# A kernel whose task order is written out as a table: the table is replaced by another one

## The chip, the cores and the metric

One core of a Trainium2 chip runs the whole program in one launch. The metric is the device time of the program in microseconds (us). Its engines are TensorE (PE, with its weight loads shown as PEld), VectorE (DVE), ScalarE (ACT), GpSimd (POOL) and SyncE (SP); each runs its own instructions strictly in the order in which they were written, and they wait for one another by semaphores.

## The reference

The output is a gated mix of two branches over a sequence of 2048 rows of 640 channels: local attention with a window of 8 keys at a stride of 2, and a long convolution whose kernel comes from a diagonal state space model.

```python
g = sigmoid((x * gate_w).sum(-1, keepdims=True))
# a: 32 heads of 20; each query sees keys at pos - 0, 2, .., 14
q, k, v = split(x @ wqkv)
logits = where(idx >= 0, einsum("bhsd,bhswd->bhsw", q, kg) * scale, -1e9)
a = (einsum("bhsw,bhswd->bhsd", softmax(logits), vg)) @ wo
# b: K = Re sum_n C_n dB_n exp(dt A_n l), 192 states per channel; FFT convolution of x with K
K = einsum("dn,dnl,dn->dl", Cc, exp(logdA[:, :, None] * l), dB).real
b = irfft(rfft(x, 4096) * rfft(K, 4096))[:2048] + x * Dskip
out = g * a + (1 - g) * b
```

## The kernel before, in words

The work is cut into 1578 tasks, each of which issues a handful of instructions on one engine. The program first builds the list of tasks with what each depends on, in a fixed numbering. Then `Plan.order` reads a table of numbers, `ORDER`, and gives the order in which the tasks are written out; there are two such tables, "main" and "tail". A number is the step from the last task's place in the list to the next one's, and a letter behind it names the engine where a task can run on either ACT (A) or DVE (D). Since every engine runs in order, the table is the whole schedule: no scheduler changes it, and the tile framework adds the semaphores that the order needs.

```python
for x in ORDER[self.name].split():
    at += int(x.rstrip("ADSG"))
    t = self.tasks[at]
    t.eng = x[-1] if x[-1] in "ADSG" else next(iter(t.dur))
    out.append(t)
```

What the tasks do, with the lines of the profile:

- Start, to about 55 us. DVE and ACT turn the model's parameters into digit pieces (tiles `pc`, L661), SP stores them to the scratch `Sprm` and reads them back as `L` tiles (L766). PE transposes x in ten tasks (L204); each is evicted from PSUM (tile `ar`) to `bufA` by ACT (L507) or DVE (L509). PE projects q, k and v in 60 groups of five matmuls (L311), each evicted from one of two PSUM buffers (`tb`) into `qA`, `kA`, `prj`, `pv` or `vst`. The gate's 80 small matmuls (L219) need all transpositions.
- Kernel generation, ten chunks. PE computes arguments (L801, tile `ar`), ACT takes Sin (L816) and Exp (L818), DVE multiplies them (L838 and L840, tiles `pt` and `qq`), PE sums the products into the chunk (L856, `kps`), and an eviction puts it into `E` ("the E eviction", L507). After five chunks a half of the kernel is expanded (`nxt`, `X`), stored to `Kx` and loaded as `kc`.
- Attention, eight slices of 256 queries, numbered 0 to 7, woven into that. DVE multiplies q by shifted k (L375, `prod`), PE sums (L381, `lg`), DVE takes the row maximum (L397 to L401), ACT Exp (L409), DVE divides (L417, L418); SP writes the result to `aS` and spreads it as `asb` (L428). POOL loads the values of a slice as `vc` in two transfers (L368) from the scratch `vS` (L344), DVE multiplies them (L449, `pv`), PE gathers (L456), and the output projection (L480) is scaled by the gate on eviction ("the gate eviction", L489 on ACT, L491 on DVE).
- Transforms. `Usb`, which is x in another layout, is loaded by POOL in eight transfers (L1004). Ahead of each but the first stands a small POOL copy that reads what the transfer before wrote (L1003, tile `pace`), so the eight run one after another. `Usb` takes the buffer in which `prj` was, so the first must wait until `prj` is no longer read. Then PE transforms `Usb` and `kc` (L1300, L1319).
- Tail, from about 267 us: the spectra (L1073), their products on DVE (L1101, L1104), the inverse transform (L1134, L1164), the mix (L1170 to L1178) and the stores (L1191).

`vc` has two buffers, which are handed out in turn in the order in which the loads are issued; a load waits until DVE has read the buffer's last contents.

## Time and profile before

| | |
|---|---|
| median of 3 runs | 336.16 us (335.34, 336.16, 339.4) |
| span of the profiled execution | 335.4 us (the page lists no other time for it) |
| PE busy | 285.5 us |
| DVE busy | 294.2 us |
| ACT busy | 293.4 us |
| POOL busy | 62.3 us |
| moved by DMA | 45.68 MB, mean 136 GB/s |

The profiled execution's span is 0.06 us above the lowest run and 0.8 us below the median. Three engines are each busy for 85 to 88% of the span, so no engine's total says what bounds the kernel. What an engine's row says of a stage must be read from that stage: its idle time, and what ended it. A PE that is busy is not a PE at its peak, since the ends of its matmuls are modelled.

### The profile page before, as it was taken

To read this page: it belongs to the slowest core of one execution; us is meant where nothing else is said; L and a number is where in the kernel's file an instruction comes from. 1 tells how busy PE (TensorE), PEld (TensorE's weight loads), DVE (VectorE), ACT (ScalarE), POOL (GpSimd) and SP (SyncE) were. 2 spreads that over 40 slices of the span, in tenths; PEclk is the share of its full clock that TensorE was granted. 3 is DMA by queue.
4 is the path that set the end of the run, shared out by engine and by line. 5 is a ranking of instruction groups with operands and counts; after the bars stand their busy time and mean duration, and the time that the engine had idled before them with its cause. 6 is when DMAs were issued, how large, how long until landed. Compare 5 with 4: busy or idle time off the path is not lost. (4 is left out here: it accounts for less than half of the span.)

```text
span 335.4 us, 11982 instructions
## 1 busy us (share of the span) xinstructions
PE 285.5 (85%) x5181; PEld 171.0 (51%) x5214; DVE 294.2 (88%) x401; ACT 293.4 (87%) x433; POOL 62.3 (19%) x94
## 2 busy tenths in 40 slices
PE   0367999997899999999998799999999899996850
PEld 0334563444445555445554344556677676665740
DVE  1997988798989999999999979999686799999881
ACT  1789736999899999999999799999987889998990
POOL 8700043020005000101412341211040000000062
PEclk9999999999999999999999989999999999999985
DMA  8984435437107110524874887365565527666056
GB/s 253 356 264 113 119 91 159 86 91 170 26 9 153 27 24 8 149 62 141 199 190 119 186 208 161 93 118 124 154 207 221 180 64 216 159 123 100 4 136 182
DMA packets 45975, 45.68 MB, mean 136 GB/s; under 512 B 25098, under 2 KB 39738, under 8 KB 45922
## 3 DMA queue, kind: packets, MB, share of 16 engines
q1 hardware_dynamic: 39928, 27.90, 30.3%
q0 software_dynamic: 5248, 16.39, 20.2%
q8 instruction: 41, 0.67, 0.9%
q10 hardware_dynamic: 746, 0.61, 0.6%
q14 instruction: 12, 0.10, 0.1%
HBM read 30.88 MB, written 14.01 MB: 134 GB/s over the span
## 5 line engine op out<-in xcount | busy, mean ns | idle before, releaser
L311 PE MATMUL tb<-bufA 128*128 128x512 bf16 x267 | 73.5, 391 | 4.2 <-issue 1.4
L816 ACT ACTIVATE big<-ar 128x740 bf16<-128x740 int16 (+1 forms) x72 | 56.7, 858 | 1.4 <-PE ar L801 1.2
L818 ACT ACTIVATE big<-ar 128x848 bf16<-128x848 f32 x60 | 50.1, 905 | 0.2
L801 PE MATMUL ar<-Rarg,L 64*128 64x212 bf16 (+4 forms) x600 | 46.5, 253 | 3.5 <-ACT big L816 1.9
L449 DVE TENSOR_TENSOR pv<-vc,asb 128x2048 bf16<-128x2048 bf16 x40 | 48.2, 1217 | 0.3 <-PE tb L456 0.3
L311 PEld LDWEIGHTS <-bufA 128*128 128x128 bf16 x300 | 31.2, 122 | 28.5 <-issue 12.3
L856 PEld LDWEIGHTS <-pt 128*32 128x32 bf16 (+1 forms) x2560 | 25.3, 92 | 35.7 <-issue 33.2
L856 PE MATMUL kps<-qq,pt 128*32 128x21 bf16 (+1 forms) x2560 | 36.6, 173 | 6.0 <-issue 5.1
L838 DVE TENSOR_TENSOR pt<-big 128x1024 bf16<-128x1024 bf16 x48 | 32.8, 701 | 4.3 <-ACT big L816 2.2
L801 PEld LDWEIGHTS <-L 64*128 64x128 bf16 x600 | 20.8, 94 | 25.2 <-issue 22.4
L480 PE MATMUL tb<-wo_sb,oT 128*128 128x320 bf16 x160 | 29.9, 306 | 0.2
L507 ACT ACTIVATE sp_u<-fp 128x640 bf16<-128x640 f32 x31 | 23.9, 953 | 0.8 <-PE fp L1073 0.8
L375 DVE TENSOR_TENSOR prod<-prj 128x2048 bf16<-128x2048 bf16 x20 | 24.0, 1218 | 0.2 <-PE lg L381 0.2
L375 DVE TENSOR_TENSOR prod<-qA,kA 128x2048 bf16<-128x2048 bf16 x20 | 23.9, 1217 | 0.2 <-PE lg L381 0.2
L507 ACT ACTIVATE sp_k<-fp 128x640 bf16<-128x640 f32 x29 | 22.6, 969 | 1.1 <-PE fp L1073 1.1
L456 PE MATMUL tb<-pv,ind 128*64 128x512 bf16 (+1 forms) x192 | 23.2, 353 | 0.0
L368 POOL DMA_DIRECT2D vc<-vS x16 | 11.5, 723 | 59.0 <-DVE pv L449 55.0
L840 DVE TENSOR_TENSOR qq<-big 128x1344 bf16<-128x1344 bf16 x24 | 21.2, 883 | 0.0
L1191 POOL DMA_DIRECT2D out_dram<-ot x14 | 7.7, 558 | 72.3 <-DVE ot L1173 72.3
L1073 PEld LDWEIGHTS <-PHI 128*128 128x128 bf16 x160 | 15.5, 97 | 8.1 <-issue 1.1
L489 ACT ACTIVATE ga<-tb,g_sb 128x320 bf16<-128x320 f32 x29 | 15.6, 550 | 3.4 <-PE tb L480 3.1
L480 PEld LDWEIGHTS <-oT 128*128 128x128 bf16 x160 | 13.1, 98 | 7.1 <-issue 3.1
(171 smaller groups left out, 547.9 us busy)
## 6 DMA issues: line engine op xcount, KB each, us to landing
vc<-vS POOLq DMA_DIRECT2D x16, 327.5 KB, 6.4
xn<-in_A_x_dram SPq DMA_DIRECT2D x4, 640.0 KB
gaS<-ga SPq DMA_DIRECT2D x8, 320.0 KB
Usb<-in_A_x_dram POOLq DMA_DIRECT2D x8, 320.0 KB, 5.7
gaF<-gaS SPq DMA_DIRECT2D x8, 320.0 KB
bufA<-in_A_wqkv_dram SPq DMA_DIRECT2D x3, 800.0 KB
Sprm<-pc SPq DMA_DIRECT2D x10, 240.0 KB
L<-Sprm SPq DMA_DIRECT2D x76, 30.0 KB
```

Source lines behind the costliest of these rows:

```text
L311: nc.tensor.matmul(ppf, self.wq[:, which, kt, e::5], self.xT[:, c0 // 1024, kt, c0 % 1024:c0 % 1024 + SC], start=(kt == 0), stop=(kt == NK ...
L375: nc.vector.tensor_tensor(b[e][:], q[:, e, o:o + C].unsqueeze(1).to_broadcast([128, W, C]), win(k[:, e, :], o, W, DIL, C), ALU.mult)
L449: nc.vector.tensor_tensor(o, vw, b["asb"][:].unsqueeze(2).to_broadcast(sh), ALU.mult)
L456: nc.tensor.matmul(b["op", e][64 * a:64 * a + 64, 0:n, :], ind[:, 32:96], b["pv", e][:, w, a, 0:n, :], start=(w == 0), stop=(w == 3), skip ...
L480: nc.tensor.matmul(apf[:, :320], b["oT"][:, e, i * 128:(i + 1) * 128], wo_sb[:, e, hf * 320:(hf + 1) * 320], start=(e == 0), stop=(e == 4))
L507: nc.scalar.activation(o, i, ACT.Identity)
L801: nc.tensor.matmul(ar[:, g2, a0:a0 + ncol], L[rows, sb, gv, l0:l0 + 128], R[rows, c0:c0 + ncol], start=True, stop=True, tile_position=(64 ...
L816: nc.scalar.activation(d_[:, :, s0 * QW:s1 * QW], ar[:].bitcast(I16)[:, :, 0:2 * (s1 - s0) * QW:2], ACT.Sin, scale=SCL)
L818: nc.scalar.activation(dst[:, gp::2].rearrange("p g s n -> p g (s n)"), ar[:, :, 0:2 * EW], ACT.Exp)
L838: nc.vector.tensor_tensor(pt[:, :, k, :], gg[:, :, ::-1] if k else gg, e1, ALU.mult)
L840: nc.vector.tensor_tensor(qq[:], trg[:, :, KI:].rearrange("p a (v m) -> p a v m", v=2), exq[:, :, KI:].unsqueeze(2).to_broadcast([128, 32, ...
L856: nc.tensor.matmul(kps[32 * g:32 * g + 32, h, NM * ql:NM * ql + NM], pt[rows, k, v, :], qq[rows, k, v, :], start=(g not in started), stop= ...
```

## The change

Both tables are replaced. The numbers of a row say nothing to a reader; the first row of "main" and of "tail" stand for all:

```diff
 ORDER = {"main": (
-    "7 -7 15 -14 1 1166 -1164 56 -57 3 2 -3 6 1 1 39 -43 1 51A -8A -25 -14 2 38 1D 1 1A -32 33 1A -42 1 69 1 -57 72 -56 57 "
+    "15 37 1116 -1161 -7 1 3 1 6 -9 1 3 48 -46 1 44 -41 48 -5 -42 48 -5 -42 2 -6 18 30 -1 2 28 1 -65 1 7 1 40 -55 5 25 42D "
...
 ), "tail": (
-    "3 1A 7 1A -7 1D 1 6 1A -6D 1 1A 10 -5 1A 1 1A 3 13 1D -13 1 1 2 1A 3 1A -3 1A -4 11 1A 6 -11 1A 11 -6 1A 1 1A -41 1 "
+    "0 13 -12 10 -4 5D 2 -6D -5 1 1 1D 14 -11 1 11 -6 1 1 1 8 1D 1 1 5 1 -33 139 -105 1 -7 1 1 1 -14 19 1 1 125 -112 -31 1 "
...
```

The tasks, their instructions, tiles and bytes are the same, and so are 19 loads of activation tables on ACT. The new table is six lines shorter, so that a line of the program has a number 6 lower in the change (L509 becomes L503). In "main", 30 evictions and parameter steps go from ACT to DVE and 23 come from DVE to ACT; in "tail", 4 go and 3 come. Three places:

DVE ahead of its first attention products (L375, then L369), from the last parameter pieces on. Before:

```order
L661 TENSOR_TENSOR pc<-at,t_144 128x960
L661 TENSOR_TENSOR pc<-t_144,t_143 128x960
L509 CAST bufA<-ar 128x1024 x3
L509 CAST kA<-tb 128x512
L375 TENSOR_TENSOR prod<-qA,kA 128x2048 x2
```

In the change:

```order
L655 TENSOR_TENSOR pc<-t_144,t_143 128x960
L503 CAST kA<-tb 128x512 x2
L503 CAST qA<-tb 128x512
L328 MEMSET kA 128x5x7
L503 CAST qA<-tb 128x512
L369 TENSOR_TENSOR prod<-qA,kA 128x2048 x2
```

The three transposition evictions (`bufA<-ar`) are gone to ACT, as is a fourth one earlier; four projection evictions stand there instead of one.

POOL between the loads of the later slices' `vc` and of `Usb`. The numbers behind the names tell the buffers apart: `vc_4160`, `vc_4812` and `vc_5174` are those of slices 4, 5 and 6. Before:

```order
L368 DMA vc_4160<-vS_68 64x10x262 x2
L1003 COPY pace_77<-Usb_3673 32x2
L1004 DMA Usb_3673<-in_A_x_dram 32x32x160
L1003 COPY pace_77<-Usb_3673 32x2
L1004 DMA Usb_3673<-in_A_x_dram 32x32x160
L938 DMA kc_4305<-Kx_178 128x2560
L1003 COPY pace_77<-Usb_3673 32x2
L1004 DMA Usb_3673<-in_A_x_dram 32x32x160
L368 DMA vc_4812<-vS_68 64x10x262 x2
L1003 COPY pace_77<-Usb_3673 32x2
L1004 DMA Usb_3673<-in_A_x_dram 32x32x160
L368 DMA vc_5174<-vS_68 64x10x262 x2
```

In the change, where `vc_4676` is slice 4's, `vc_5097` slice 5's, `vc_5107` slice 7's and `vc_5578` slice 6's, from the fifth load of `Usb` on:

```order
L362 DMA vc_4676<-vS_68 64x10x262 x2
L997 COPY pace_77<-Usb_3956 32x2
L998 DMA Usb_3956<-in_A_x_dram 32x32x160
L997 COPY pace_77<-Usb_3956 32x2
L998 DMA Usb_3956<-in_A_x_dram 32x32x160
L997 COPY pace_77<-Usb_3956 32x2
L998 DMA Usb_3956<-in_A_x_dram 32x32x160
L1001 DMA omF_76<-omS_58 32x32
L987 DMA PHI_4864<-c_phi 128x1536
L932 DMA kc_4862<-Kx_178 128x2560
L1001 DMA omF_76<-omS_58 32x32 x2
L362 DMA vc_5097<-vS_68 64x10x262 x2
```

Slice 5's values now come behind all eight loads of `Usb` and five other transfers. Behind them follow `vc_5107` (slice 7) and `vc_5578` (slice 6), in this order.

DVE at the end of the kernel products, around the last value product of slice 5 (`pv` with 128x8x256) and the first of slice 6. Before:

```order
L417 RECIPROCAL rs_5293<-lg_4734 128x64
L418 TENSOR_TENSOR at_5218<-at_5218,rs_5293 128x512
L449 TENSOR_TENSOR pv_104<-vc_4812,asb_5029 128x8x256
L838 TENSOR_TENSOR pt_5470<-bufA_78,big_601 128x32x32 x2
L840 TENSOR_TENSOR qq_5471<-bufA_78,big_601 128x1344
L449 TENSOR_TENSOR pv_104<-vc_5174,asb_5335 128x4x512 x3
```

In the change:

```order
L443 TENSOR_TENSOR pv_104<-vc_5097,asb_4857 128x8x256
L832 TENSOR_TENSOR pt_5227<-big_585 128x32x32
L834 TENSOR_TENSOR qq_5228<-big_585 128x1344
L832 TENSOR_TENSOR pt_5301<-big_585 128x32x32 x2
L834 TENSOR_TENSOR qq_5302<-big_585 128x1344
L832 TENSOR_TENSOR pt_5355<-bufA_78,big_585 128x32x32 x2
L834 TENSOR_TENSOR qq_5356<-bufA_78,big_585 128x1344
L411 RECIPROCAL rs_5409<-lg_5047 128x64
L412 TENSOR_TENSOR at_5264<-at_5264,rs_5409 128x512
L485 TENSOR_SCALAR ga_5407<-tb_5347,g_sb_65 128x320
L443 TENSOR_TENSOR pv_104<-vc_5578,asb_5160 128x4x512 x4
```

The last softmax division (`rs`, `at`) stands behind the kernel products instead of ahead of them, and the work between slice 5's last value product and slice 6's first has grown from one kernel product to nearly three.

88 rows, old and new, of the table ORDER are left out of this document.

## The prediction

> **What bounds the kernel now.** I read the page first, then the span cut into its stages, then the groups of instructions with their idle time, and last the timelines of VectorE (DVE), ScalarE (ACT), TensorE (PE) and GpSimd (POOL) at the places where something waits.
>
> ```profile
> span 335.4 us, 11982 instructions
> PE 285.5 (85%) x5181; PEld 171.0 (51%) x5214; DVE 294.2 (88%) x401; ACT 293.4 (87%) x433; POOL 62.3 (19%) x94
> 55.00:100.00 45.00, 40.80 (x772) 20.38 (x785) 38.66 (x56) 42.70 (x60) 4.03 (x6) 1.00 0.38 85
> 100.00:188.00 88.00, 84.02 (x1933) 44.62 (x1950) 85.50 (x119) 87.85 (x134) 15.68 (x25) 1.00 0.46 110
> 188.00:196.00 8.00, 5.64 (x99) 2.15 (x96) 5.75 (x7) 5.58 (x10) 3.50 (x3) 0.79 0.74 180
> 196.00:232.00 36.00, 34.61 (x956) 19.63 (x952) 35.15 (x45) 35.67 (x53) 9.52 (x13) 1.00 0.57 132
> 232.00:267.00 35.00, 32.77 (x326) 24.68 (x326) 27.81 (x40) 30.42 (x45) 4.37 (x8) 1.00 0.63 200
> ```
>
> The columns of a stage are its length and the busy time of PE, weight loads, DVE, ACT and POOL. No engine is the bound alone. From 55 to 232 ACT is busy 171.8 of 177 us (42.70 + 87.85 + 5.58 + 35.67) and DVE 165.1. What an order can win lies in DVE's idle time before 100, in the hole at 188 to 196, and in the stage 232 to 267, where PE has the least idle time (35.00 - 32.77 = 2.2). The chain that ended last covers only the final stores and says nothing of the change.
>
> Where DVE waits before 100, and the hole at 191:
>
> ```profile
> 44.89 0.69 DVE L509 CAST kA<-tb 128x512 bf16<-128x512 f32 x1 [0.72 <-PE tb L311]
> 49.06 0.69 DVE L509 CAST prj<-tb 128x512 bf16<-128x512 f32 x1 [0.43 <-PE tb L311]
> 62.31 0.69 DVE L509 CAST prj<-tb 128x512 bf16<-128x512 f32 x1 [1.33 <-PE tb L311]
> 76.74 1.34 DVE L509 CAST prj<-tb 128x512 bf16<-128x512 f32 x2 [1.73 <-PE tb L311]
> 94.44 0.69 DVE L509 CAST prj<-tb 128x512 bf16<-128x512 f32 x1 [1.16 <-PE tb L311]
> 191.39 0.27 PE L856 MATMUL kps<-qq,pt 128*32 128x21 bf16 x15 [2.36 <-issue]
> 194.26 0.71 DVE L838 TENSOR_TENSOR pt<-big 128x1024 bf16<-128x1024 bf16 x1 [2.25 <-ACT big L816]
> ```
>
> The bracket is the idle time just before and who ended it. DVE stands still because an eviction of a projection was put on it before PE had made the projection. The hole is PE's own (nothing that the profile shows held it) and DVE loses 2.25 us by it. The order cannot aim at that hole; I leave it in.
>
> **The change part by part.** The instructions and bytes are the same, so each term is work that goes to another engine or a wait that goes or comes. The prices of what changes engine:
>
> ```profile
> L509 DVE CAST prj<-tb 128x512 bf16<-128x512 f32 x10 | 6.8, 688 | 5.8 <-PE tb L311 5.8
> L491 DVE TENSOR_SCALAR ga<-tb,g_sb 128x320 bf16<-128x320 f32 x3 | 1.6, 546 | 1.0 <-ACT big L507 1.0
> L509 DVE CAST bufA<-ar 128x1024 bf16<-128x1024 f32 x4 | 4.7, 1215 | 0.0
> L507 ACT ACTIVATE prj<-tb 128x512 bf16<-128x512 f32 x15 | 9.3, 636 | 1.4 <-PE tb L311 1.4
> L489 ACT ACTIVATE ga<-tb,g_sb 128x320 bf16<-128x320 f32 x29 | 15.6, 550 | 3.4 <-PE tb L480 3.1
> L507 ACT ACTIVATE E<-kps 128x336 bf16<-128x336 f32 x10 | 4.7, 471 | 1.3 <-PE kps L856 1.3
> L507 ACT ACTIVATE nxt<-nxp 128x320 bf16<-128x320 f32 (+1 forms) x4 | 1.5, 472 | 0.0
> L645 DVE TENSOR_SCALAR x<-tau 128x960 f32<-128x960 f32 x2 | 1.3, 651 | 0.0
> 231.39 0.89 DVE L840 TENSOR_TENSOR qq<-bufA,big 128x1344 bf16<-128x1344 bf16 x1
> ```
>
> *The start, up to DVE's first product.* The four transposition evictions leave DVE (4.7 us) and two projection evictions with them; six other projection evictions and two parameter steps come (6 x 0.69 + 2 x 0.65 = 5.4 us, against 4.7 + 1.4 that leave), so DVE's work there is nearly as before. But the last projection that DVE now evicts ahead of its first product is made by PE behind the gate's 80 matmuls, and these wait for the last transposition.
>
> ```profile
> 44.69 2.14 PE L219 MATMUL ar<-gw_sb,bufA 128*128 128x1 bf16 x80
> 46.69 2.33 PE L311 MATMUL tb<-bufA 128*128 128x512 bf16 x9
> 48.95 0.61 PE L381 MATMUL lg<-prod,ind 128*32 128x512 bf16 x8
> 52.07 0.40 PE L381 MATMUL lg<-prod,ind 128*32 128x512 bf16 x4
> 52.40 1.11 PE L311 MATMUL tb<-bufA 128*128 128x512 bf16 x4
> 53.88 1.28 ACT L816 ACT_TABLE_LOAD   x1 [2.87 <-PE ar L801]
> ```
>
> Until now DVE evicted the last three transpositions one after another (3 x 1.2) behind its last parameter piece; ACT, which hands off as much as it takes over, can put them between its projections. I put the gate at 42 instead of 44.7. Then 2.1 for the gate, ten L311 matmuls at 2.33 / 9 each (2.6) and an eviction of 0.69 put the first product at about 47, 1.5 later than its 45.49 (which follows the 44.89 row by 0.6). Bounds: 0, if PE comes in time, and 3, if the gate starts no earlier than now. In exchange the first trigonometric argument has 4 L311 and 12 L381 matmuls fewer ahead of it on PE (1.11 + 0.61 + 0.40 = 2.1), so ACT's Sin stage starts 2.1 earlier than 53.88. That helps only if DVE keeps up.
>
> *From the first product to the last kernel product* (the L840 row at 231.39, which ends at 232.3). On DVE one projection eviction fewer (-0.69), two gate evictions more (+1.09), three E evictions (DVE has no such row: between the 0.47 of ACT and the 0.69 of DVE for 512 columns in place of 336; I take 0.5, near the first: +1.5), the nxt copy of two pieces (on ACT 2 x 0.47: +0.9), and one softmax division moved behind this stage (-1.24): +1.6 by the means, and +1.3 as neighbours overlap. The waits: of those above, 0.43 and 1.16 belong to evictions that go to ACT; the 1.73 now has three 1.2 us products ahead of it and goes; the 1.33 has another product ahead and loses 1.2. With 0.5 of small waits, -5.0; the bounds are -2.3 (only the first two and the smallest) and -8 (all before 100). Sum to here: +1.5 + 1.3 - 5.0 = -2.2, with ends of +1 and -7.
>
> *POOL's queue.* This is the new wait to fear. Eight loads of Usb stand in a chain: each is preceded by a small copy that waits until the load before has landed. Until now a vc load stood between most of them; now the vc load for query slice 5 stands behind all eight and five other transfers. (The line on landing is that of the vc loads, from issue to landed.)
>
> ```profile
> 159.08 0.82 POOL L1004 DMA_DIRECT2D Usb<-in_A_x_dram  x1 [5.00 <-DVE hi L400]
> 165.55 0.42 POOL L1003 COPY pace<-Usb 32x2 bf16<-32x2 bf16 x1 [4.23 <-DMA Usb<-in_A_x_dram]
> 172.01 0.73 POOL L1003 COPY pace<-Usb 32x2 bf16<-32x2 bf16 x1 [4.66 <-DMA Usb<-in_A_x_dram]
> 181.97 0.25 POOL L1003 COPY pace<-Usb 32x2 bf16<-32x2 bf16 x1
> 189.85 2.20 POOL L1003 COPY pace<-Usb 32x2 bf16<-32x2 bf16 x1 [6.89 <-DMA Usb<-in_A_x_dram]
> 197.06 1.18 POOL L1003 COPY pace<-Usb 32x2 bf16<-32x2 bf16 x1 [3.71 <-DMA Usb<-in_A_x_dram]
> 203.41 0.43 POOL L1003 COPY pace<-Usb 32x2 bf16<-32x2 bf16 x1 [3.00 <-DMA Usb<-in_A_x_dram]
> 198.99 1.43 POOL L368 DMA_DIRECT2D vc<-vS  x2
> DMA to landing us min/median/max: 4.4/6.4/7.3
> 220.32 1.22 DVE L449 TENSOR_TENSOR pv<-vc,asb 128x2048 bf16<-128x2048 bf16 x1
> ```
>
> A free step took 6.5, 6.5, 7.9, 7.2 and 6.4 us (differences of the rows, leaving out the one that a vc load held). The chain starts when the last product that reads the old tile is done, which now stands 4.2 us of work later on DVE; with the 2.2 won I put it at 157.5 instead of 159.1. Seven steps of 6.5 lead to 203.0; the last copy and load (0.4 + 0.8), the five transfers (0.5 to 0.6 each) and the first of the two vc issues (0.7) take 4.6 more, and 6.4 to land: 214.0. DVE's work from its first use of that tile to the end of the stage is 12.0 us now (220.3 to 232.3); in the new order two logit products (1.2 each), a row maximum (1.1) and two kernel products (0.6 each) come into it and the division (1.2) goes: 15.3. At the pace above DVE arrives at 232.3 - 2.2 - 15.3 = 214.8. The load is in time by 0.8: a wait of 0. With steps of 6.9 (their mean) it is 2.0 late. Further on, the vc load for slice 6 must wait for the end of slice 5's last product, since the load for slice 7 has taken the free buffer; DVE has some 7.2 us of other work in between, the load needs 0.72 + 6.4 = 7.1, up to 8.0: 0 to 0.8, taken as 0.
>
> One sentence from the Trainium skill speaks against this part: "SBUF — State Buffer", section "SBUF: two separate sides", says that a busy VectorE can lock GpSimd out while it writes descriptors, and its subsection on bandwidth pools gives 3.1 us for an issue that takes 0.62 alone. By that the vc pair above would be some 5 us late (an estimate from that page). The trace does not agree for these issues, 1.43 us for two beside a full DVE; only the small POOL copies swing, from 0.25 to 2.20.
>
> *Stage 232 to 267.* DVE's work grows by about 1 (the division above), ACT's stays, PE's is the same transforms and projections. DVE idles 7.2 here, but PE only 2.2, so the gain lies between 0 and 2.2; as two big evictions come ahead of the stage on ACT and DVE's gate evictions stand together at its end, I take 1.5. *Tail.* Three spectrum evictions go to DVE and two come back (0.82 for one), the multiplications stand as before: 0, between -1.5 and +0.8.
>
> Sum: -2.2 - 1.5 = -3.7 on the profiled span of 335.4, so 331.7. The median of the runs is 336.16, 0.8 above that span; I take the same distance: **332.5 us**.
>
> **The rivals.**
> *More is won.* All of DVE's early waits go and ACT decides. For ACT: Sin 2.1 earlier; between first Sin and last E eviction one projection eviction, two gate, three E evictions and a copy less (0.62 + 1.08 + 1.41 + 0.95 = 4.1), and the 1.27 that stood before the first E eviction: -7.5; the stage behind gives its 2.2. That is 336.2 - 9.7 = 326.5. For it: ACT is full from 55 on. Against: DVE gets 1.3 more work in that stage and is as full after 100.
> *Nothing is won.* The first product comes 3 late, the waits removed come back before other evictions, and the two cancel: 336. For it: the projections come from the same two PSUM buffers.
> *POOL's chain decides, slower than before.* The chain runs without a break beside the stores and loads of the first kernel half; if its steps take 7.9, the longest above, and vc 7.3 to land, slice 5's tile comes 7 x 1.4 + 0.9 = 10.7 later than 214.0, at 224.7, and DVE, which runs its queue in order, waits 9.9 on the product that needs it. 332.5 + 9.9 = 342.4. It costs from steps of 6.6 on and turns the gain into a loss from about 7.1. Against it: three of five steps were 6.5 or less.
>
> **How the numbers follow.** Forecast 0.52, more won 0.22, nothing won 0.13, POOL slower 0.13. The forecast's own spread is 329 to 335.5. The range 326.5 to 340 takes in the two middle cases, all of the larger gain but its lower tail, and POOL's chain up to steps of 7.5. About 2%, or 6.7 us, is what a measurement here can tell from no change: faster than 329.4 are most of the larger gain and the lower edge of the forecast, 0.27; slower than 342.9 is nearly half of POOL's case and some unforeseen wait, 0.10; within, 0.63.
>
> **What would show it.** Right: the first Sin's table load near 51.8; idle time before DVE's prj evictions down from 5.8 to under 2; slice 5's first product near 215 with under 1 us of idle time; the last kernel product ending near 230; a stage of 33 us behind it. Wrong: a wait of several us of a pv product on a vc load (the chain), DVE's first product past 48.5, or more than 69 us behind that stage. The forecast falls as a whole if DVE shows more idle time between 47 and 230 than before.

## The result, and the profile after

The change is slower: 348.02 us, the median of 4 runs (346.32 to 349.4), against 336.24 (335.34 to 339.4) for the kernel before, a ratio of 1.0337 (95% interval 1.0277 to 1.0398). The forecast of 332.5 and its range (326.5 to 340) are missed on the far side. Medians are of all runs of a kernel; ratios leave out those that were over 1.5% above its fastest.

The page of the change, its first lines, the row of the queue that brings instructions (packets, MB, share of the DMA engines), and from the view of the cores the mean granted clock:

```profile
span 347.3 us, 11967 instructions
PE 292.7 (84%) x5192; PEld 176.7 (51%) x5214; DVE 296.3 (85%) x410; ACT 292.8 (84%) x424; POOL 63.6 (18%) x94
q8 instruction: 40, 0.66, 0.8%
...
core 0: 347.3 us, clock 0.952
```

The tasks are the same, so the 11.9 us between the two spans (347.3 - 335.4) are waits and slower matmuls, but for what evictions cost on another engine. The mean clock is 0.952 (before 0.980). Of the page's 40 slices it is below nine tenths in nine; before, the only slice of the middle that fell was the one that begins at 193 us. The same stages as in the prediction (length, busy time of PE, weight loads, DVE, ACT, POOL, granted clock, DMA share, GB/s):

```profile
55.00:100.00 45.00, 42.38 (x821) 21.34 (x827) 40.84 (x58) 41.65 (x57) 2.31 (x3) 0.96 0.29 67
100.00:188.00 88.00, 80.51 (x1879) 42.88 (x1886) 78.87 (x117) 79.30 (x115) 13.13 (x22) 0.94 0.35 86
188.00:196.00 8.00, 7.52 (x175) 4.08 (x172) 8.00 (x10) 8.00 (x15) 2.72 (x4) 1.00 0.73 158
196.00:232.00 36.00, 30.55 (x668) 16.57 (x667) 30.83 (x35) 32.54 (x49) 12.07 (x13) 0.95 0.73 187
232.00:267.00 35.00, 32.24 (x491) 23.34 (x489) 30.29 (x47) 29.94 (x41) 4.23 (x7) 0.95 0.49 148
```

Up to 100 DVE gained, as forecast (40.84 busy in place of 38.66). From 100 to 188 it lost 6.6 us of work (78.87 for 85.50) and ACT 8.6, and at 196 to 232 again 4.3 and 3.1; at 188 to 196, where the kernel before has its hole, they gained 2.3 and 2.4. By milestones: DVE's first product starts at 45.8 (45.5 before), the last kernel product ends at 240.0 (232.3), the tail begins at 277.9 (266.6) and is 69.4 long (68.8). So 0.3 us are lost up to the first product, 7.4 from there to the last kernel product, 3.6 in the stage behind it, 0.6 in the tail. The test that the prediction named for its fall, the same stretch of before and then of the change:

```profile
47.00:230.00 183.00, 171.22 (x3731) 89.18 (x3760) 169.88 (x231) 171.83 (x254) 32.92 (x47) 0.99 0.47 112
```
```profile
47.00:230.00 183.00, 166.64 (x3565) 87.44 (x3583) 162.92 (x224) 167.01 (x240) 36.23 (x51) 0.95 0.43 105
```

DVE idles 20.1 us there in place of 13.1. What the idle time is spent on shows best near 180: the change's timeline of PE and ACT, then two windows.

```profile
177.32 2.06 PE L850 MATMUL kps<-qq,pt 128*32 128x21 bf16 x192
181.33 0.49 PE L795 MATMUL ar<-Rarg,L 64*128 64x74 bf16 x4 [1.96 <-issue]
181.92 0.79 ACT L810 ACTIVATE big<-ar 128x740 bf16<-128x740 int16 x1 [2.51 <-PE ar L795]
```
```profile
178.00:181.00 3.00, 1.37 (x132) 1.19 (x130) 3.00 (x5) 1.41 (x3) 0.97 (x2) 0.93 0.49 71
181.00:187.00 6.00, 5.67 (x37) 1.76 (x37) 2.99 (x5) 3.77 (x6) 0.28 (x1) 0.50 0.32 87
```

PE runs 192 small sums (eight tasks, four of 16 and four of 32) in 2.06 us, then does nothing for 1.96 us though nothing that the profile shows holds it ("issue"); its clock is 0.50 for 6.8 us from 180.6 on; ACT waits 2.51 for its arguments, and DVE is busy 2.99 of 6 us. The same, smaller, at 81 and 160:

```profile
81.32 0.22 PE L850 MATMUL kps<-qq,pt 128*32 128x21 bf16 x7 [1.37 <-issue]
82.00 1.47 ACT L810 ACTIVATE big<-ar 128x740 bf16<-128x740 int16 x2 [1.83 <-PE ar L795]
159.54 0.23 PE L850 MATMUL kps<-qq,pt 64*32 64x21 bf16 x9 [0.86 <-issue]
164.77 2.42 ACT L812 ACTIVATE big<-ar 128x848 bf16<-128x848 f32 x3 [3.41 <-PE ar L795]
```

Between 55 and 262 us all holes of this kind over 0.6 us stand at one place of PE's instruction stream. If PE's weight loads are numbered from 0, each stands ahead of a number that is 93 modulo 128, or ahead of the matmul just before it (I call this place a border); 128 weight loads and their 128 matmuls are 256 instructions, and q8 above brings 40 pieces of 0.66 MB / 40 = 16 KB. Counted from the records of the trace, groups of 128 weight loads between 55 and 262 us: the shortest time for its first 127, and the stop behind them.

```
                 last 127 loads / stop, us (at)
before           3.19/0.00 (202)   4.37/2.55 (191)   4.76/2.11 (84); no other group under 3.8
the change       1.11/1.18 (125)   1.15/2.14 (181)   1.55/1.56 (81)   1.79/1.05 (160)   then 3.37/0.02 (109)
```

(For the stop at 125 the timeline names ACT as well, with 0.86.) Added up, PE's pauses of over 0.2 us at these borders are 6.5 us in the change and 5.1 before, so the time of the holes by itself is not the loss.

The two orders differ in what makes such groups. A task of sums issues 16 or 32 of the small matmuls (L850). Before, never more than two such tasks follow one another on PE; the change has 14 runs of four, one of eight (at 177.3) and one of seven.

Two transfers are late as well. The eight loads of `Usb` (ns of one: least, median, most; first and last start), POOL's queue, the landing row of `vc`, and DVE where it waits for slice 5's values, with DVE's work at 210:

```profile
L998 POOL DMA_DIRECT2D Usb<-in_A_x_dram x8: 784/788/831, 158.9 to 211.0; - x8
207.04 4.03 POOL L997 COPY pace<-Usb 32x2 bf16<-32x2 bf16 x1 [5.53 <-DMA Usb<-in_A_x_dram]
214.41 1.46 POOL L362 DMA_DIRECT2D vc<-vS  x2
DMA to landing us min/median/max: 4.4/6.0/9.1
209.70 1.32 DVE L832 TENSOR_TENSOR pt<-big 128x1024 bf16<-128x1024 bf16 x2
210.94 0.55 DVE L411 RECIPROCAL rs<-lg 128x64 f32<-128x64 f32 x1
224.52 1.23 DVE L443 TENSOR_TENSOR pv<-vc,asb 128x2048 bf16<-128x2048 bf16 x1 [4.69 <-DMA vc<-vS]
```

The copy of four bytes a row took 4.03 us; it began beside DVE's products, which read SBUF twice, and ended at 211.07, as DVE turned to a RECIPROCAL out of PSUM. Slice 5's pair was issued at 214.41, its product began 10.1 us later, and DVE had stood there for 4.69. In the stage behind, the second half of the kernel is expanded late and its `kc` comes late:

```profile
252.80 0.65 POOL L923 DMA_DIRECT2D Kx<-X  x1 [16.81 <-DVE X L897]
268.89 0.42 PE L1313 MATMUL tb<-F1k,kc 128*128 128x256 bf16 x2 [3.65 <-DMA kc<-Kx]
270.06 1.23 DVE L503 CAST big<-bp 128x1024 bf16<-128x1024 f32 x1 [4.24 <-PE bp L1294]
```

### The profile page after: what moved, and what is told of

It is laid out like the page before. It is cut to its first block, busy times and chain, and to the rows that moved or that the text cites. A ratio compares the mean times of both kernels' runs of the same rounds, so it can differ in the third digit from the quotient of the medians.

```text
span 347.3 us, 11967 instructions
## 1 busy us (share of the span) xinstructions
PE 292.7 (84%) x5192; PEld 176.7 (51%) x5214; DVE 296.3 (85%) x410; ACT 292.8 (84%) x424; POOL 63.6 (18%) x94
## 5 line engine op out<-in xcount | busy, mean ns | idle before, releaser
L305 PE MATMUL tb<-bufA 128*128 128x512 bf16 x278 | 75.0, 400 | 5.8 <-ACT bufA L501 2.8
L795 PE MATMUL ar<-Rarg,L 64*128 64x212 bf16 (+4 forms) x600 | 48.5, 257 | 8.4 <-issue 2.0
L443 DVE TENSOR_TENSOR pv<-vc,asb 128x2048 bf16<-128x2048 bf16 x40 | 47.4, 1219 | 7.9 <-DMA vc<-vS 4.7
L305 PEld LDWEIGHTS <-bufA 128*128 128x128 bf16 x300 | 32.8, 122 | 34.2 <-issue 15.0
L850 PEld LDWEIGHTS <-pt 128*32 128x32 bf16 (+1 forms) x2560 | 23.5, 92 | 13.9 <-issue 12.1
L850 PE MATMUL kps<-qq,pt 128*32 128x21 bf16 (+1 forms) x2560 | 27.7, 175 | 2.9 <-issue 2.9
L474 PE MATMUL tb<-wo_sb,oT 128*128 128x320 bf16 x160 | 28.0, 311 | 0.0
L501 ACT ACTIVATE sp_k<-fp 128x640 bf16<-128x640 f32 x29 | 24.2, 1008 | 1.5 <-PE fp L1067 1.5
L450 PE MATMUL tb<-pv,ind 128*64 128x512 bf16 (+1 forms) x192 | 24.9, 381 | 0.0
L369 DVE TENSOR_TENSOR prod<-qA,kA 128x2048 bf16<-128x2048 bf16 x20 | 23.9, 1219 | 0.4 <-PE lg L375 0.4
L369 DVE TENSOR_TENSOR prod<-prj 128x2048 bf16<-128x2048 bf16 x20 | 23.8, 1218 | 0.1
L1067 PEld LDWEIGHTS <-PHI 128*128 128x128 bf16 x160 | 15.5, 97 | 8.1 <-issue 1.1
L474 PEld LDWEIGHTS <-oT 128*128 128x128 bf16 x160 | 14.6, 100 | 7.3 <-issue 2.7
L375 PE MATMUL lg<-prod,ind 128*32 128x512 bf16 x160 | 15.6, 407 | 2.7 <-DVE prod L369 2.1
```

What stands on the lines that cost most here:

```text
L305: nc.tensor.matmul(ppf, self.wq[:, which, kt, e::5], self.xT[:, c0 // 1024, kt, c0 % 1024:c0 % 1024 + SC], start=(kt == 0), stop=(kt == NK ...
L369: nc.vector.tensor_tensor(b[e][:], q[:, e, o:o + C].unsqueeze(1).to_broadcast([128, W, C]), win(k[:, e, :], o, W, DIL, C), ALU.mult)
L443: nc.vector.tensor_tensor(o, vw, b["asb"][:].unsqueeze(2).to_broadcast(sh), ALU.mult)
L450: nc.tensor.matmul(b["op", e][64 * a:64 * a + 64, 0:n, :], ind[:, 32:96], b["pv", e][:, w, a, 0:n, :], start=(w == 0), stop=(w == 3), skip ...
L474: nc.tensor.matmul(apf[:, :320], b["oT"][:, e, i * 128:(i + 1) * 128], wo_sb[:, e, hf * 320:(hf + 1) * 320], start=(e == 0), stop=(e == 4))
L501: nc.scalar.activation(o, i, ACT.Identity)
```

## The experiments

My first theory was the two late transfers (vc 4.7, kc 4.2); the rival was PE's bursts of sums. Times are medians, and ratios are against the kernel before on the same chip. Each kernel is another order of the same tasks, but for matmuls added where that is said.

**The late transfers.** x_early expands the second half of the kernel at once, ahead of the last three value products of a slice; vc_order issues slice 5's load ahead of the eighth load of `Usb` instead of behind it and five other transfers, and slice 6's ahead of slice 7's; sum_spread issues the sums one task at a time; all_three does all of it.

```diff
 # DVE, x_early
-L443 TENSOR_TENSOR pv<-vc,asb 128x4x512 x4
-L443 TENSOR_TENSOR pv<-vc,asb 128x8x256
-L503 CAST oT<-tb 128x512
+L443 TENSOR_TENSOR pv<-vc,asb 128x4x512 x2
 L882 TENSOR_TENSOR E<-E,Dk 128x80
 L897 COPY X<-E 128x640
...
 # POOL, vc_order
 L998 DMA Usb<-in_A_x_dram 32x32x160
+L362 DMA vc<-vS 64x10x262 x2
 L997 COPY pace<-Usb 32x2
 L998 DMA Usb<-in_A_x_dram 32x32x160
...
 L1001 DMA omF<-omS 32x32 x2
-L362 DMA vc<-vS 64x10x262 x6
+L362 DMA vc<-vS 64x10x262 x4
```

> The changed order with one repair: the second kernel half is expanded (shift, X copies, store to Kx) right after its last E eviction instead of 6.5 us later, so that kc can land before PE asks for it. Theory 'transfers' (the loss comes from late vc and kc loads): the 3.65 us wait of PE on kc at 268.9 and the 4.24 us idle of DVE behind it go, 348.0 becomes 343.5. Theory 'bursts' (the loss comes from runs of four to eight kernel-sum matmul tasks on PE, which empty its instruction supply and leave windows of low activity after which the granted clock is 0.5): PE's bursts are untouched and the wait on kc only hid other waits of that stage, so at most 2 us are won, 346 or more, and the windows at 0.5 before 240 stay.

> The changed order with another repair: on POOL the values of slice 5 are loaded after the seventh Usb load instead of behind the eighth and five further transfers, and slice 6 before slice 7. 'Transfers': the 4.69 us wait of DVE at 224.5 goes; DVE and ACT lost 2.9 us on average there, so 345. 'Bursts': the wait stood beside PE's slow windows anyway, at most 1 us is won, 347.

> The changed order with the kernel-sum tasks (32 weight loads and 32 small matmuls each) spread one at a time between PE's other tasks instead of in runs of four to eight; nothing else moves. 'Bursts': the holes at 80, 159 and 180 and the windows at clock 0.5 behind them go (four of the seven windows), DVE and ACT idle 6 to 8 us less on average, 348.0 becomes 341. 'Transfers': the waits on vc and kc decide, whatever PE wins before 220 is given back there: 346 to 348.

> The three repairs together on the changed order. If both theories hold and add: 348.0 - 4.5 - 3 - 7 = 333.5, a little under the time before. If 'transfers' alone: 340.5. If 'bursts' alone: 341. If the loss has a third source, the time stays above 343.

The branch "transfers" asked for 343.5 and 345. x_early took 348.07 (1.0312, 1.0273 to 1.0352) and vc_order 346.99 (1.0304, 1.0262 to 1.0346): 0 and 1 us, though the waits they aimed at are gone (that of PE for kc in x_early, that of DVE for slice 5's vc in vc_order). Others stand in their place. In x_early's timeline:

```profile
182.93 0.49 PE L795 MATMUL ar<-Rarg,L 64*128 64x74 bf16 x4 [3.62 <-issue]
255.74 0.55 DVE L485 TENSOR_SCALAR ga<-tb,g_sb 128x320 bf16<-128x320 f32 x1 [3.39 <-DMA gaS<-ga]
258.29 1.23 DVE L443 TENSOR_TENSOR pv<-vc,asb 128x2048 bf16<-128x2048 bf16 x1 [2.00 <-DMA asb<-aS]
```

The stores of the kernel now stand ahead of `asb` and `gaS` on SP. So the late transfers are real, but each alone is worth about 1 us at most, and my first theory fell. sum_spread (357.11; 1.0578, 1.0541 to 1.0616) and all_three (358.88; 1.0625, 1.0566 to 1.0685) made it worse: I had put the sums so early that PE stood before products that were not there, as here in sum_spread, and everything behind on PE's queue with it.

```profile
86.69 0.27 PE L852 MATMUL kps<-qq,pt 128*32 128x21 bf16 x16 [1.97 <-DVE E L505]
```

**Where along the program.** Grafts: the first N tasks in the sequence of one table, the rest in that of the other, cut at 69, 131 and 175 us of the change and at 178 us of before; and before with its sums gathered into runs of four.

```diff
 # after_to_N: tasks of "main"
-change[0:all]
+change[0:N] + [t for t in before if t not in change[0:N]]
...
 # before_fours: tasks of PE, in each group of a chunk
-sum 0 ... sum 1 ... sum 2 ... sum 3
+... ... ... sum 0, sum 1, sum 2, sum 3
```

> The order before with one edit: the four kernel-sum tasks of each of the 30 groups, which stood one or at most two at a time between PE's other tasks, are all put at the place of the last of the four, as the changed order has them for 14 groups. 'Bursts' (runs of kernel-sum tasks outrun PE's instruction supply and leave windows of low activity): more holes of 1 to 3 us in PE with no releaser and more windows at clock 0.5, 336.5 becomes 341 to 344. Rival (the runs are harmless, a group only needs its last sum): 336.5 within 1.5, with no more than one window at 0.5 before 300.

> A graft: the changed order up to the place where its run is at 131 us (580 of 1274 tasks), then what is left in the sequence before. 'Late stages' (the changed order is no worse up to there, its loss comes behind): its start is 1.3 and its stage 55 to 75 is 0.7 us better, the hole at 80 costs 0.6, so 335.5, within 1.5 of the order before. 'Bursts': its runs of four before 131 each open a hole, and the holes at 80 and 123 already cost: 338 to 340.

> The reverse graft: the order before up to 178 us (800 tasks), then the rest in the changed sequence. It has the changed order's run of eight kernel sums at 177, slice 5's late vc load and the late expansion of the second kernel half. Idle time of DVE and ACT that the changed order shows there above the order before: 0.8 at 180 to 190, 2.9 + 0.7 at 220 to 240, 3.4 at 240 to 280, 7.8 in all. 'Late stages': 336.5 + 7.8 = 344. 'Bursts' alone, spread over the whole span: half of the 12 us, 341 to 342.

> The graft with the cut at 69 us (240 of 1274 tasks): the changed order's start, which had 2.0 us less idle time of DVE and ACT up to 75, without its hole at 80; then the order before. If the better start is carried to the end: 335.0 to 335.5 against 337.1, a ratio of 0.995. If the stages behind take it back, as in the graft at 131: 1.000 within 0.004.

> The same graft at 175 us (800 tasks). Against the graft at 131 it adds the hole at 159 and the window at 0.5 behind it, in which DVE and ACT lost 3.2 us: 338.5 to 339 if that hole belongs to the order and not to one execution. If the loss lies behind 175 (late vc and kc), it stays at 335.5 to 336.5.

```
                                 us     ratio (95%)
change up to  69, then before  333.46  0.9906 (0.9870 to 0.9942)
change up to 131, then before  336.86  0.9993 (0.9946 to 1.0040)
change up to 175, then before  340.60  1.0081 (1.0039 to 1.0123)
change                         348.02  1.0337 (1.0277 to 1.0398)
before up to 178, then change  351.16  1.0381 (1.0274 to 1.0489)
before, its sums in fours      345.43  1.0246 (1.0153 to 1.0339)
```

The start of the change is a gain of its own: with it alone the kernel beats both, by 0.9%.

```profile
span 331.7 us, 11981 instructions
```

Each further piece costs 3.4, 3.7 and 7.4 us, and brings short groups with it (none under 3 us at 69, those at 82 and 124 at 131, that at 160 at 175). A piece holds more than its sums, so this says where and not yet what. Nor do the pieces add up: before_to_178 was to take 344, or 341 to 342, and at 351.16 it is slower than the change itself, though its first 178 us are those of before. In its trace the run of eight is followed by a hole of 3.12 us (at 184) and by 10.2 us at half clock. after_to_175 has the change's holes at 82, 124 and 159 (1.56, 1.00 and 0.98), but no half clock behind them in its profiled execution, which at 337.26 was the fastest of its ten. before_fours, at 345.43 a little above the 341 to 344 that the bursts asked for, says less than it seems to: it has one hole, of 1.92 us, and what grew is DVE's wait to write `pt` until PE has summed, since gathered sums free that buffer later. From its waits, and then from those of before (in total, times, longest):

```profile
DVE pt L836 <- PE kps L854: 8.8, 10, 2.5
```
```profile
DVE pt L838 <- PE kps L856: 1.6, 5, 0.4
```

**PE's supply by itself.** burst_alone runs matmuls behind the whole kernel, when nothing else moves: 48 large, 1024 small, 48 large, then 32 times (32 small, 3 large). They write a spare PSUM tile that nothing reads.

```diff
+    dense(48)
+    small(1024)
+    dense(48)
+    for i in range(32):
+        small(32)
+        dense(3)
```

> The order before, with idle PE work behind the whole program whose results nothing reads: 48 dense matmuls (128x128 weights, 512 columns), 1024 small ones like those of the kernel sums (32 columns of weights each, 21 columns moved, 2048 instructions with the weight loads), 48 dense, then 32 times 32 small and 3 dense. It measures PE's instruction supply alone. 'Supply': in the changed order 384 such instructions took 2.06 us, 5.4 ns each; the run of 2048 goes at that pace for 400 to 500 instructions and then stops about every 256 for a fetch, so it takes 16 us or more instead of 11, with holes of about 1 us; the clock is at 0.5 in the windows inside it although PE is busy, since the small matmuls fill little of the array, and the mixed part runs without holes at clock 1. Rival (the holes in the kernel come from DMA traffic that delays a fetch, not from the run): no holes, since no DMA runs there, 11 us.

Its timeline, and then two windows, the first of the small matmuls and the second of the mix:

```profile
339.02 1.78 PE L1204 MATMUL yp<-psi 128*32 128x21 bf16 x199
343.36 1.20 PE L1204 MATMUL yp<-psi 128*32 128x21 bf16 x128 [2.56 <-issue]
365.73 0.63 PE L1204 MATMUL yp<-psi 128*32 128x21 bf16 x57 [2.24 <-issue]
```
```profile
344.00:348.00 4.00, 1.47 (x179) 1.38 (x171) 0.00 (x0) 0.00 (x0) 0.00 (x0) 0.50 0.01 4
384.00:388.00 4.00, 3.82 (x138) 1.83 (x140) 0.00 (x0) 0.00 (x0) 0.00 (x0) 1.00 0.01 4
```

128 matmuls with their weight loads, 256 instructions, go in 1.20 us, and then PE stands 2.2 to 2.6 us, with the DMA share at 0.01 and nothing to wait for. The 1024 took 27 us (from 339.0 to 366.4), where I had expected 16 or more. The mix, 138 matmuls in 4.00 us, had no hole. So with nothing else moving, the supply is 256 instructions in 3.5 to 4 us. The clock is 0.50 in the run of small matmuls and 1.00 in the mix; whether the stops or the small matmuls lower it, these rows do not tell (PE is busy 1.47 of 4.00 us in one and 3.82 in the other).

What PE waits for is in the DMA records. Here are burst_alone's transfers at 343.4 to 344.6 and at 344.6 to 345.6, and then before's queues at 184.5 to 188.5, without q8, and q8 at 188.5 to 190.1:

```profile
DMA packets 0, 0.00 MB, mean 0 GB/s; under 512 B 0, under 2 KB 0, under 8 KB 0
q8 instruction: 1, 0.02, 5.5%
```
```profile
q0 software_dynamic: 153, 0.51, 68.3%
q1 hardware_dynamic: 335, 0.19, 30.4%
q8 instruction: 1, 0.02, 5.7%
```

In burst_alone a piece of 16 KB starts 1.2 us after PE has passed a border (at 343.4), takes 0.9, and PE goes on 1.6 us after it has landed: 3.7 us in all. All 20 traces agree. Each of the 83 holes of over 0.5 us at a border between 55 and 262 us ends 1.2 to 1.7 us after a piece has landed, and at none of the 627 borders there does PE go on sooner. A piece starts 0.9 us (median) after PE has passed the last border, at the extremes 1.7 ahead and 4.8 behind. It starts late where other transfers are dense: 0.6 us where the share of the DMA engines in the 2 us behind the border is under 0.3, and 2.5 where it is 0.9 or more (medians). So there are two ways to a hole. The change's four at 81, 125, 160 and 181 follow groups that PE ran through in less than a piece needs (their pieces started at 0.84 us or less). Those of before at 84 and 191 follow longer groups whose pieces started only 4.08 and 4.06 us after the border; the share of the DMA engines in those 4 us was 0.88 and 0.99.

**Moving the holes without touching the order.** shift_20 and shift_108 put 20 or 108 small matmuls on zeros ahead of the change's first work on PE: every border of 256 instructions then lies that many matmuls earlier in the program. split_eight pulls the run of eight apart, and four_repairs does that with both repairs of transfers, and puts one sum of logits behind work that is ready. before_eight makes a run of eight in the kernel before. split_all breaks all runs but the one of seven, split_all_more adds the repairs of transfers to that, and split_shift is split_eight with the 20 matmuls.

```diff
 # shift_20, ahead of PE's work
+    for _ in range(20):
+        nc.tensor.matmul(zk[0:32, 0, 0:21], at.zf[:, 0:32], at.zf[:, 32:53], start=True, stop=True)
...
 # split_eight: tasks of PE from 177 us
-sum 0, sum 1, sum 2, sum 3, sum 4, sum 5, sum 6, sum 7
+sum 0 ... sum 1 ... sum 2 ... sum 3 ... sum 4, sum 5, argument, sum 6 ... sum 7
...
 # before_eight: the same eight tasks
-sum 0 ... sum 1 ... sum 2 ... sum 3 ... sum 4 ... sum 5 ... sum 6 ... sum 7
+... ... ... sum 0, sum 1, sum 2, sum 3, sum 4, sum 5, sum 6, sum 7
```

> The changed order with one edit on PE: the eight kernel-sum tasks in a row at 177 us are put one at a time between the matmuls ahead (last projection, arguments, output projection) and behind (arguments, logits). 'Bursts': the hole of 2 to 3.6 us that stood behind this run in all four kernels that have it goes, with the 6.8 us at clock 0.5 behind it; DVE and ACT lost 3.5 us on average there: 348.0 becomes 344.5. Rival (PE would stop there anyway, as the order before stops at 191): 347 to 348, the hole moves by some us.

> The changed order with four edits: the eight sums split as above; slice 5's values loaded ahead of the eighth Usb load and slice 6 before slice 7; the second half expanded at once, its SP store still behind the asb loads; and the last logit sum of slice 7 (which waits for its product) behind the value sums and arguments that are ready. If these are the causes behind 175 us: 3.5 + 2.9 + 3.4 + 1.5 = 11 off 348.0, about 337 to 338. If each wait removed is taken by another, no more than 3 us: 345.

> The changed order with its kernel-sum tasks spread one at a time (one run of seven before the last E eviction stays), but gently: none earlier than 2 us after its products and 2.5 us before its old place, where the first attempt put them as early as 0.8 us behind their products and made PE wait. If the runs of four behind the one of eight are what is left of the loss: 337 to 340. If only the run of eight counts: 343, as with that one split. If a sum that comes later than planned costs more than a run: above 345.

> The same, and slice 5's values earlier, the second kernel half expanded at once, the last logit sum behind ready work. If late transfers cost time once PE is fed: 3 to 5 us below split_all. If not: within 1.5 of it.

> The order before with the eight kernel-sum tasks of chunk 6, which stand between 179.4 and 186.8 us one or two at a time, put in one row at 183.1 us; no other task moves. 'Supply': a hole of 2 to 4 us in PE behind the row and windows at clock 0.5, 337.2 becomes 340 to 342 (the hole at 191 may go in exchange, then 338). Rival (in the changed order the hole was due to the DMA traffic there): 337.2 within 1.

> The changed order, with 20 small dummy matmuls on PE (and their weight loads) ahead of its first work, while PE is idle; nothing reads them. All later instructions of PE stand 40 places further on, so the borders between its groups of 256 fall elsewhere. By the times of the weight loads in the changed order's trace, two groups instead of four would then take under 2 us (at 77 and 174; those at 120 and 154 no longer). 'Supply' (a group that takes less than about 3.4 us is followed by a wait for the next): holes at 120 to 125 and 157 to 161 gone, 348.0 becomes 343 to 345. Rival (the holes belong to the order or to the DMA traffic at their place): they stay where they were, 347 to 349.

> The same with 108 dummy matmuls: by the same count five groups would take under 2 us (at 91, 120, 139, 155 and 233), and what they lack of 3.4 us sums to 11.0 us instead of 8.0 in the changed order and 5.5 with 20 dummies. 'Supply': holes near 93, 122, 141, 157 and 236, none at 80 and 180, 350 to 352. Rival: as the changed order, 347 to 349, and equal to the kernel with 20 dummies.

> The run of eight sums split and 20 dummy matmuls. One group under 2 us is left (at 78), the lack sums to 4.3 us. If both repairs act on the same cause and add: 340 to 341, half of the loss and more taken back; what is then left above 337 belongs to other waits. If the shift does nothing: 343.2.

```
                  us     ratio (95%)                 with the change itself at 348.02
shift_20        342.40  1.0125 (1.0051 to 1.0199)    a little faster than 343 to 345
split_eight     343.16  1.0207 (1.0154 to 1.0260)    -4.9, about as expected
four_repairs    343.75  1.0225 (1.0173 to 1.0276)    nearer to 345 than to 337: no more than split_eight
shift_108       344.46  1.0189 (1.0132 to 1.0245)    miss: faster, not slower
split_shift     350.74  1.0402 (1.0350 to 1.0454)    miss: slower
split_all       352.86  1.0461 (1.0367 to 1.0556)    slower: the branch "above 345"
split_all_more  354.20  1.0492 (1.0401 to 1.0584)    as split_all: earlier transfers won nothing
before_eight    337.90  1.0023 (0.9978 to 1.0068)    no cost: not the 340 to 342 of the supply
```

The holes moved, in the main as the count foretold. In shift_108 those at 123, 144, 161 and 237 were foretold, and those at 182 and 215 were not; the one foretold at 93 did not come. In shift_20's timeline the hole at 81 is down to 0.62; the 128 sums that in the change were cut into 119, a stop and 9 run through; and another hole stands at 179 (its piece started 2.7 us after the border):

```profile
81.49 0.34 PE L851 MATMUL kps<-qq,pt 128*32 128x21 bf16 x27 [0.62 <-issue]
156.12 1.18 PE L851 MATMUL kps<-qq,pt 64*32 64x21 bf16 x128
179.48 0.32 PE L851 MATMUL kps<-qq,pt 64*32 64x21 bf16 x20 [3.95 <-issue]
```

And matmuls that compute nothing made the kernel 5.6 us faster (7.1 by the ratios), a thing that no account by waits on tiles or transfers gives; by the ratios split_eight won 4.4. A run of eight need not cost anything. In before_eight a border happens to cut it (122 sums, 0.46 of pause, 70 more), and the hole at 191, 2.36 us before, is down to 0.3; I had named this exchange, with 338:

```profile
182.04 1.18 PE L856 MATMUL kps<-qq,pt 128*32 128x21 bf16 x122
183.67 0.69 PE L856 MATMUL kps<-qq,pt 64*32 64x21 bf16 x70 [0.46 <-issue]
```

What goes with the time better than the holes' sum is the time at half clock between 55 and 275 us, read from the clock records of the profiled executions (correlation with the span 0.72, and 0.36 for the holes). A profiled execution is up to 7 us from its kernel's median, so a span goes with the windows of its own execution.

```
                span   half clock, us (windows at)           holes, us
change to 69    331.7    3.4 (189)                              2.1
before_eight    332.7    0                                      2.8
change to 175   335.0    3.4 (192)                              5.9
before          335.4    3.4 (192)                              5.1
change to 131   336.2    6.8 (124, 193)                         4.7
shift_108       340.1   10.2 (123, 215, 263)                    7.7
four_repairs    342.4   17.1 (124, 196, 213)                   10.7
before_fours    342.8    6.8 (204)                              2.0
shift_20        343.8   17.1 (178, 215, 239, 267)               9.6
vc_order        344.8   17.1 (82, 181, 215, 242)               11.2
x_early         346.2   20.5 (82, 181, 202, 222, 243)          10.8
change          347.3   23.9 (82, 160, 181, 218, 232, 269)      6.5
split_shift     347.5   13.7 (81, 207, 225)                     2.0
split_eight     348.7   17.1 (82, 127, 222, 270)                6.2
split_all       350.0   10.2 (129, 207, 228)                    7.5
before_to_178   350.8   20.5 (85, 180, 245, 273)                5.7
split_all_more  354.8   20.5 (129, 187, 228, 252, 269)          5.7
sum_spread      355.6   13.7 (168, 206, 226)                    7.0
all_three       357.3   13.7 (89, 171, 208, 232)                9.0
```

Orders in which the sums were gathered or spread do not fit (before_fours, split_shift, split_all, sum_spread, all_three); something else decides there. In split_shift I take it to be POOL. Its timeline, DVE's beside it, and one of two waits of 7.4 us of value products, which the profile puts down to `vc`:

```profile
178.93 15.79 POOL L998 COPY pace<-Usb 32x2 bf16<-32x2 bf16 x1 [3.78 <-DMA Usb<-in_A_x_dram]
190.05 4.62 DVE L444 TENSOR_TENSOR pv<-vc,asb 128x2048 bf16<-128x2048 bf16 x4
194.59 0.68 DVE L392 TENSOR_REDUCE mx<-lg 128x64 f32<-128x512 f32 x1
DVE pv L444 <- DMA vc<-vS: 7.4, 1, 7.4
```

The small copy stood 15.79 us and ended at 194.72, as DVE's row of products gave way to a reduction out of PSUM at 194.59. My reading, which no run tested, is that with no hole of PE at 181 DVE had work without a break, and that POOL's chain came that much later for it. Being busy is not all: in the change the copy at 180.01 took 0.47 beside a DVE that was busy without a break. split_eight's profiled execution, 7 us longer than its median, has a long copy too:

```profile
190.66 8.16 POOL L997 COPY pace<-Usb 32x2 bf16<-32x2 bf16 x1 [1.27 <-DMA Usb<-in_A_x_dram]
```

So the repairs do not add up, if this reading is right because less waiting for PE means later transfers. Why split_all and split_all_more lose as much as they do is not settled; PE's own holes are back in both (7.4 us of waiting for "issue" ahead of sums in split_all), so one at a time is no remedy either.

## Why the prediction was wrong, step by step

- **The start** was right in sign, and better than its size: the first Sin's table load came at 49.91 (51.8 forecast, 53.88 before), the first product at 45.8 (47 forecast, 45.5 before; the bound for failure was 48.5). The gain up to 100 was real and smaller: DVE idles 5.8 us between 47 and 100 in place of 7.5. The graft at 69 shows it by itself: 333.46, near the 332.5 that I gave to the whole.
- **DVE's projection evictions** wait 3.5 us in place of 5.8, not under 2:

```profile
L503 DVE CAST prj<-tb 128x512 bf16<-128x512 f32 x8 | 5.5, 686 | 3.5 <-PE tb L305 3.5
```

- **The step that failed** is the sentence "The order cannot aim at that hole; I leave it in." I had the mark of the mechanism in a row, a PE that stops for 2.36 us on "issue" right at a small sum (L856), followed by a clock of 0.79, and put no price on it. That hole came of a piece of instructions that started 4.06 us after the border, beside dense transfers. The order decides both ways to such a hole: how many small sums follow one another, and which transfers stand beside a border. My sums took every PE task as a fixed duration that other engines see only when they wait for it, so a denser order of PE's small matmuls was free. In the change PE ran through four groups in 1.1 to 1.8 us and stopped behind each, and the time at half clock grew from 3.4 to 23.9 us. Pulling one run apart gave back 4.9 of the 11.8 us, and moving the borders 5.6.
- **POOL's queue** is the term that was mis-sized. I said that the load of slice 5 would be in time by 0.8; DVE waited 4.69. Its last load of `Usb` (784 ns at least) was issued at 211.0, which ends at 211.8; my sum had 204.2. Of the 7.6 us between, 1.4 are the start of the chain (158.9 for 157.5), 3.6 the last copy, which stood 4.03 where I took 0.4, and 2.6 its other steps. The pair was issued at 214.41, by my sum 206.9, and its product began 10.1 us later, for which I took 7.1 (0.7 + 6.4). The sentence of the Trainium skill that I weighed there ("SBUF — State Buffer", "SBUF: two separate sides") I set aside for the issues, and the trace still agrees with that (1.46 for two); the page gives its 3.1 us for a DMA beside a copy on VectorE, which I read as the issue. I did not carry its rule over to the copies, though the row of 2.20 stood there. The rival "POOL's chain decides" thus named a real wait, with half its size (4.69 of 9.9) and a sign that came true, but not the cause: without that wait the kernel takes 346.99.
- **Stage 232 to 267** was forecast to win 1.5 and lost 3.6 (37.9 in place of 34.3): `kc` is late for PE by 3.65. Taking that wait away won nothing.
- **The tail** was right: 69.4 for 68.8, within the +0.8 that was allowed, though past the 69 that I named as a sign.
- **Sums.** Three are a little off: the first product's terms give 47.4 and not 47, the upper end up to the last kernel product is +2 and not +1 (3 + 1.3 - 2.3), and DVE's work ahead of slice 5's product is 15.5 and not 15.3. A run's time stands 1.7 us above its span (349.04 for 347.3), and I took 0.8. None of these is what failed.

Shown: that the holes stand at borders of 256 PE instructions and end when the next piece has come, that a run of small sums makes them without any other load, that matmuls on zeros move them and take 5.6 us off, that pulling apart the run of eight takes off 4.9, that the late transfers alone are worth 0 to 1 us, and that the start is a gain. Open: how the 11.8 us divide between the stop, the half clock behind it and the transfers, since each repair uncovers the next; what sets off a half clock; and why the spread orders are slow. An estimate for the half clock, from the runs: over 148 executions, each against the mean of its kernel, 1 us more at half clock goes with 0.26 us more span (taken as twice what the mean clock lacks of 1, times the span; correlation 0.73). The change's four average 28.0 us at half clock over the whole span, before's 15.0, so by that rate about 3 of the 11.8 us.

## What to carry to other kernels

When an order is searched with traced durations, an engine's own limits are not in the durations: count the instructions that an order puts on PE in any 4 us, and price a run of its smallest matmuls that exceeds some 250 instructions in 4 us, and dense transfers beside a border of 256; spreading all of the sums blindly was slower still. An unexplained stop in the trace of before ("issue") is a price to be found before the forecast, not a constant. And repairs of single waits must be tried together and alone: here one wait stood behind another, and a queue beside a fuller engine came later.

## What the runs showed of the hardware

PE's instructions come in pieces of 256, with nothing else moving one each 3.5 to 4 us: 1.20 us of small matmuls, then 2.2 to 2.6 us of nothing. A piece is on its way from about when PE passes into the one before it, 0.9 us after the border in the median and up to 4.8 beside dense transfers, and PE goes on 1.2 us or more after it has landed. The Trainium skill, "Runtime: NRT & Kernel Launch", section "Instruction fetch mechanics", has the same blocks of 16 KiB or 256 instructions, and says that fetching the next is mostly hidden. The size agrees with the 16 KB of q8; the hiding holds at most borders here, and not at those 83 holes.

The clock of 0.50 lasts 3.41 us or a multiple of it (6.83 at 181, 10.24 in before_to_178, 27.31 in burst_alone), but for the last one of a kernel, and within an execution all its starts are whole multiples of 3.41 us apart. It also follows stretches in which PE was far from idle: in the change PE was busy 2.17 of the 3.40 us up to 180.6 and 2.54 of those up to 160.1. What sets it off is open.

A POOL copy of 32x2 took from 0.17 to 15.79 us, beside DVE's products; the long ones ended as DVE turned to an instruction that reads PSUM (at 210.94 in the change, 194.59 in split_shift). The Trainium skill's "SBUF — State Buffer", section "Who interferes with whom", says that a VectorE instruction with two SBUF inputs and a GpSimd instruction that reads SBUF exclude one another for a whole instruction. The long copies agree on who excludes whom, but the one of 15.79 us stayed out over a row of some twenty such instructions, not one; and the copy of 0.47 at 180.01, between two of them, shows that it need not.
